# Four staging buffers for the second MoE's weights, and each weight conversion split into two queued steps

## The chip, the cores and the metric

The kernel runs on one core of one Trainium2 chip. The metric is device time in microseconds (us) of one execution, the median of several runs. The engines are named as in the profile: PE is TensorE (matmuls, with PEld for its weight loads), ACT is ScalarE, DVE is VectorE, POOL is GpSimd and SP is SyncE, which here only issues DMAs. Each engine works through its own queue in order; semaphores join the queues.

## What is computed

Three stages in float32: a delta-rule attention, a dense MLP, and a soft mixture of 8 experts in which every token goes through every expert. The change touches the third stage (D = 384, E = 8 experts, F = 1024, N = 3072 tokens).

```
def _moe2_ref(x, w_gate, w1, w2) -> np.ndarray:
    N, D = x.shape
    E = w_gate.shape[1]
    logits = x @ w_gate
    ...
    for e in range(E):
        h = np.maximum(x @ w1[e], 0.0)
        ye = h @ w2[e]
        out += P[:, e:e + 1] * ye
    return out.astype(np.float32)
```

`P` is the gate, normalised over rows and columns eight times (a Sinkhorn iteration).

## The kernel before

**Order of the work.** Attention and the first MLP run interleaved over six time steps of 512 tokens. The second MoE then runs in three passes (`p`) of 1024 tokens (two time steps each), each over 8 experts (`e`), each over 4 groups (`k`) of 256 hidden columns. `groups` lists these 96 triples and `n` numbers them.

**Precision.** Every float32 operand is held as two float16 halves, high and low, and a product is made of three matmuls (high-high, high-low, low-high). A Strassen-like scheme makes each 2x2 block product out of 7 products on sums of blocks; therefore each group's first weights need four sums of blocks beside the six blocks themselves.

**One expert on PE.** `prod` gives each group 11 products of three matmuls of 512 columns (33; 132 for an expert). `second` gives each of 8 token blocks 24 matmuls of 384 columns (192 for an expert). ACT copies out of PSUM (`copied`, L975) and makes high halves of the hidden values (`hi`, L990), DVE adds (`mixed`, L980), makes low halves (`lo`, L994) and accumulates each finished token block into `acc` (`flush`, L1061). For the first expert of a pass `flush` is a plain copy on ACT instead (L1056).

**Preparing weights.** While PE computes the 8 token blocks of one expert, the weights of the next are converted: four tasks `make_w1` and four `make_w2`, in turn, one at each `prep.now()` behind a block's `flush`. A task's raw float32 weights are brought by a DMA from `wc` into a staging tile `stg` (L790 or L807, issued by SP). `make_w1` then has ACT scale them in place (`scaled`, L750), POOL make the four sums (L799, which write into the same tile), ACT write the high half in two pieces (L801) and POOL the low half in two pieces (L802). `make_w2` is a scale, a high half (L813) and a low half (L814). All of ACT's instructions here go through `ordered`, which fixes them in program order; a `stg` tile comes free when POOL's last piece of the task has read it.

**The queue of tasks.** `Stage.fetch` starts loads until two tasks are loaded; `staging` has two buffers. `Stage.step` fetches, converts the oldest loaded task and fetches again. At the last group of an expert (`k == 3`) the tasks of the next expert are added. At the last expert of the first two passes (`edge`) two tasks more are added, which load the next pass's two blocks of `x` (L741, 768 KB each) and split and sum them (`make_xo`: `pair` and the sums in `xsum`, ACT L754, DVE L764 and L755). These instructions of `make_xo` do not go through `ordered`: the scheduler of the framework places them between the others.

**Where PE meets the conversion.** In the next expert's first group, PE makes products in PSUM bank `ph` (`self.x`), ACT copies it (`x1 = copied(self.x, "xc", 1)`), PE goes on with banks `y` and `z`, and then accumulates into `ph` again (`fifth`), for which the copy must have been made. On ACT that copy stands in the queue behind all of the conversions.

Of the kernel before, what the change touches and what calls it, by code (L numbers as in the profile page):

```python
# [8 lines left out]
F32 = mybir.dt.float32  # L9
# [11 lines left out]
NT = S // C  # L21
NP = H // 2
DM = H * D
KD = DM // 128
FF1 = 2048
NF1 = FF1 // 128
E = 8
# [3 lines left out]
TB = B * C  # L31
# [5 lines left out]
W1R, W2R = 6, 8  # L37
# [15 lines left out]
def delta_moe_kernel(ctx: ExitStack, tc: tile.TileContext, k_l, v_l, q_l, beta_l, wa_in, wg, wc, out):  # L53
# [324 lines left out]
    class Background:  # L378
        def __init__(self):
            self.threads = deque()  # L380
            self.active = deque()
            self.credit = 0.0

        def add(self, key, fn, after=()):
            self.threads.append((key, fn, after))
# [34 lines left out]
        def pending(self):  # L420
            return bool(self.active or self.threads)
# [203 lines left out]
    if True:  # L625
# [102 lines left out]
        w1o = [[wr_p.tile([128, 9, 128], F16, name=f"w1{n}{i}") for n in "hl"] for i in range(W1R)]  # L728
        w2o = [[wr_p.tile([128, 2, DM], F16, name=f"w2{n}{i}") for n in "hl"] for i in range(W2R)]
        cst_p = ctx.enter_context(tc.tile_pool(name="cst", bufs=2, side="right", reuse_waits="tile"))  # L730
# [3 lines left out]
        gx = [gx_p.tile([128, KD, TB], F32R, name=n) for n in ("gxh", "gxl")]  # L734

        def staging():
            return cst_p.tile([128, KD * TB], F32, tag="stg", name="stg", bufs=2)

        def load_x(t):
            s = staging().rearrange("p (c n) -> p c n", c=KD)  # L740
            sp.dma_start(out=s, in_=x2_dram[t].rearrange("c p n -> p c n"))  # L741
            return s
# [6 lines left out]
        def scaled(x, col):  # L749
            ordered(act.activation(out=x, in_=x, func=ACTF.Copy, scale=scl[:, col:col + 1]))  # L750

        def pair(hi, lo, src, col):
            sc = scl[:, col:col + 1]
            act.activation(out=hi, in_=src, func=ACTF.Copy, scale=sc)  # L754
            dve.scalar_tensor_tensor(out=lo, in0=src, scalar=sc, in1=hi, op0=ALU.mult, op1=ALU.subtract)  # L755

        def make_xo(s, t):
            i, col, xo = t % 2, 2 * E + t, xos[t // 2 % 2]
            b11, b12 = s[:, 0, 0:256], s[:, 0, 256:512]
            b21, b22 = s[:, 1, 0:256], s[:, 1, 256:512]  # L760
            tt = cst_p.tile([128, 4, 256], F32, tag="xsum", name="xsum", bufs=1)
            for o, x, y in ((tt[:, 0], b12, b11), (tt[:, 1], b22, tt[:, 0]), (tt[:, 2], b22, b12),
                            (tt[:, 3], b21, tt[:, 1])):
                dve.tensor_tensor(out=o, in0=x, in1=y, op=ALU.subtract)  # L764
            for j, src in ((slice(0, 1), s[:, 0:1, 0:256]),
                           (slice(1, 5), s[:, 1:3].rearrange("p c (n k) -> p (c n) k", n=2)), (slice(5, 9), tt)):
                if j.stop - j.start > 1:
                    for n in range(j.start, j.stop):
                        pair(xo[0][:, n, i], xo[1][:, n, i], src[:, n - j.start], col)
                else:  # L770
                    pair(xo[0][:, j.start, i], xo[1][:, j.start, i], src[:, 0], col)
                yield

        groups = [(p, e, k) for p in range(NT // 2) for e in range(E) for k in range(NF2 // 2)]
# [3 lines left out]
        def ordered(ins):  # L778
            e = ins.ins.engine
            if e in last_of:  # L780
                tc.add_manual_dep(ins.ins, last_of[e].ins.name, mybir.DependencyInfo(
                    mybir.DependencyClass.NoSync, mybir.DependencyReason.DATA), reason="as written")
            last_of[e] = ins
# [3 lines left out]
        def load_w1(n):  # L787
            _, e, k = groups[n]
            s = staging()[:, 0:1280].rearrange("p (j f) -> p j f", f=128)
            sp.dma_start(out=s[:, 0:6].rearrange("p (j c) f -> p j (c f)", j=2),  # L790
                         in_=wc[e, 2 * k:2 * k + 2, :, 0:DM].rearrange("j p c -> p j c"))
            return s

        def make_w1(n, s):
            hi, lo = w1o[n % W1R]
            scaled(s[:, 0:6], groups[n][1])
            for o, x, y, op in ((6, 3, 4, ALU.add), (7, 6, 0, ALU.subtract), (8, 0, 3, ALU.subtract),
                                (9, 1, 7, ALU.subtract)):
                pool.tensor_tensor(out=s[:, o], in0=s[:, x], in1=s[:, y], op=op)  # L799
            for j, i in ((slice(0, 3), slice(0, 3)), (slice(3, 9), slice(4, 10))):  # L800
                ordered(act.activation(out=hi[:, j], in_=s[:, i], func=ACTF.Copy))  # L801
                pool.tensor_tensor(out=lo[:, j], in0=s[:, i], in1=hi[:, j], op=ALU.subtract)  # L802
# [6 lines left out]

        def make_w2(n, s):  # L810
            hi, lo = w2o[n % W2R]
            scaled(s, E + groups[n][1])
            ordered(act.activation(out=hi, in_=s, func=ACTF.Copy))  # L813
            pool.tensor_tensor(out=lo, in0=s, in1=hi, op=ALU.subtract)  # L814


        class Stage:
            def __init__(self):
                self.tasks, self.loaded = deque(), deque()

            def add(self, load, make, arg):
                self.tasks.append((load, make, arg))

            def fetch(self):
                while self.tasks and len(self.loaded) < 2:
                    load, make, arg = self.tasks.popleft()
                    self.loaded.append((make, arg, load(arg)))

            def step(self):
                self.fetch()  # L830
                if self.loaded:
                    make, arg, s = self.loaded.popleft()
                    g = make(arg, s)
                    self.fetch()
                    if g:
                        yield from g

            def now(self):
                for _ in self.step():
                    pass  # L840

        prep = Stage()

# [8 lines left out]
        def pre_c():  # L852
            yield from powers(0, NSC, bank)
            for t in (2, 3, 4, 0, 1):
                prep.add(load_x, early_x, t)
                if t > 1:
                    prep.add(load_w1, make_w1, t - 2)
                    prep.add(load_w2, make_w2, t - 2)
            prep.add(load_w1, make_w1, 3)
            prep.add(load_w2, make_w2, 3)  # L860
            prep.fetch()
            yield
            yield
            while prep.loaded:
                yield from prep.step()
                yield
            last_of.clear()
# [86 lines left out]
            for c in range(KD):  # L954
                parts(g5[0][:, c], g5[1][:, c], s[:, c], dve)

        prep.add(load_x, late_x, NT - 1)
        prep.now()
        bgq.add("sink", sinkhorn)

# [23 lines left out]
        class Group:  # L984
# [24 lines left out]
            def second(self):  # L1009
                prod(self.x, self.n, [(7, 7)], False)  # L1010
                mixed(self.x, self.q, out=self.q)
                self.c[1, 0] = mixed(self.w, self.q)
# [54 lines left out]
        for n, (p, e, k) in enumerate(groups):  # L1067
            g = Group(n)
            edge = e == E - 1 and p < NT // 2 - 1
            if k == NF2 // 2 - 1:  # L1070
                for j in range(n + 1, min(n + 5, len(groups))):
                    if edge and j < n + 3:
                        prep.add(load_x, lambda t, s: make_xo(s, t), 2 * p + 1 + j - n)
                    prep.add(load_w1, make_w1, j)
                    prep.add(load_w2, make_w2, j)
                prep.fetch()

            g.first(prev)
            if prev:
                prev.second()  # L1080
            g.third(prev)
            if prev:
                prev.fourth()
            g.fifth(prev)
            prev = g
            if k < NF2 // 2 - 1:
                continue
            prev = None
            ps = [ye_p.tile([128, 512], F32, tag="ye", name="ye") for _ in range(2)]
            g.hi(0, 1)  # L1090
            second(ps[0], n, 0, range(NF2 - 2))
            g.second()
            g.lo(0, 1)
            g.hi(1, 0)
            g.lo(1, 0)
            second(ps[1], n, 1, range(NF2 - 2))
            g.fourth()
            g.hi(1, 1)
            g.lo(1, 1)
            for blk in range(2 * B):  # L1100
                if blk < 2:
                    second(ps[blk], n, blk, range(NF2 - 2, NF2))
                    y = ps[blk]
                else:
                    y = ye_p.tile([128, 512], F32, tag="ye", name="ye")
                    second(y, n, blk, range(NF2))
                flush(y, p, e, blk)
                for _ in range(2 if edge and blk < 2 else 1):
                    prep.now()
# [45 lines left out]
```

## Time and profile before

| what | value |
|---|---|
| median of 3 runs | 2574.31 us (2574.07 to 2576.93) |
| the profiled execution: its own time | 2581.06 us |
| its span (first to last instruction) | 2579.3 us |
| mean granted PE clock in it | 0.938 of full speed |
| PE matmul busy | 2315.1 us (90% of the span) |
| ACT busy | 1395.7 us (54%) |
| DVE busy | 1330.6 us (52%) |
| POOL busy | 849.7 us (33%) |

Durations below come from the profiled execution; its own time is 6.75 us above the median of the runs. A busy share is an average over the whole span: the second MoE begins at about 945 us and takes the rest.

### The profile page before, as it was taken

Reading aid. Unit: us, or ns where it says so; the run is one execution under the profiler, and the core shown is the slowest. Engines: PE = TensorE matmul, PEld = TensorE weight load, DVE = VectorE, ACT = ScalarE, POOL = GpSimd, SP = SyncE. Lnnn points to the kernel's source line nnn. Section 1 sums busy time; section 2 is a strip of 40 time slices with the busy share of each in tenths; the row PEclk is TensorE's granted clock in tenths of the full one; section 3 lists DMA queues with packets and bytes.
Section 4 is the critical chain, followed back from the end, with each engine's and each line's share of the span. In section 5 each row is a group of like instructions: output and inputs, shape, how many; then the busy total and the mean of one; then the engine's idle time right before and its main releaser. Section 6 shows DMA issues by size and latency. Waiting matters only on the chain.

```text
span 2579.3 us, 36179 instructions
## 1 busy us (share of the span) xinstructions
PE 2315.1 (90%) x13842; PEld 1454.1 (56%) x13842; DVE 1330.6 (52%) x2529; ACT 1395.7 (54%) x2445; POOL 849.7 (33%) x966
## 2 busy tenths in 40 slices
PE   6888899899999888898999799999998899999998
PEld 5776778677778654444454344444444444444454
DVE  8667867676642557434444545444434443444444
ACT  6887665656554645445445555454555554454543
POOL 5435211333322313333333233333333333333330
PEclk7678999999899999999999899999999999999999
DMA  3355665555443631111111221111112311111110
GB/s 114 129 167 174 220 211 164 196 175 189 149 137 113 226 106 50 50 50 42 44 50 48 63 61 38 49 50 49 50 50 62 86 50 50 50 49 39 49 50 25
DMA packets 127133, 240.05 MB, mean 93 GB/s; under 512 B 13552, under 2 KB 98160, under 8 KB 126960
## 3 DMA queue, kind: packets, MB, share of 16 engines
q1 hardware_dynamic: 126960, 237.75, 29.6%
q8 instruction: 108, 1.77, 0.3%
q14 instruction: 65, 0.53, 0.1%
HBM read 215.59 MB, written 22.02 MB: 92 GB/s over the span
## 4 chain that ended last, share of the span: by engine, by line
PE 52%; ACT 15%; DMA 11%; POOL 11%; DVE 7%; issue 3%; POOLq 0%; ACTq 0%; SPq 0%; DVEq 0%
PE ye L1048 13%; PE ph L965 12%; DMA stg<-wc 7%; PE w L965 6%; POOL stg L799 5%; POOL w1l L802 5%; PE ph L550 4%; PE y L965 3%; PE z L965 3%; PE po L602 3%; ACT stg L750 3%; DMA wraw<-wc 2%; PE y_ps L355 2%; PE w_ps L346 2%; ACT w1h L801 1%
## 5 line engine op out<-in xcount | busy, mean ns | idle before, releaser
L799 POOL TENSOR_TENSOR stg<-stg 128x128 f32<-128x128 f32 x384 | 171.2, 467 | 1080.1 <-ACT stg L750 1051.3
L965 PEld LDWEIGHTS <-w1h 128*128 128x128 f16 x2112 | 213.1, 101 | 394.9 <-issue 174.2
L1061 DVE SCALAR_TENSOR_TENSOR acc<-ye,pm,acc 128x384 f32<-128x384 f32 x168 | 103.4, 617 | 430.9 <-PE ye L1048 430.9
L965 PE MATMUL ph<-xoh,w1h 128*128 128x512 f16 x480 | 190.5, 397 | 127.6 <-ACT xc L975 122.0
L750 ACT ACTIVATE stg<-stg,scl 128x768 f32<-128x768 f32 x192 | 177.7, 926 | 222.8 <-DMA stg<-wc 222.8
L802 POOL TENSOR_TENSOR w1l<-stg,w1h 128x384 f16<-128x384 f32 x192 | 245.8, 1280 | 7.7
L602 PE MATMUL po<-gh,w 128*128 128x512 f32 (+1 forms) x600 | 218.0, 407 | 4.9 <-ACT gh L590 4.9
L801 ACT ACTIVATE w1h<-stg 128x384 f16<-128x384 f32 x192 | 131.1, 683 | 137.5 <-POOL stg L799 134.5
L550 PE MATMUL ph<-x1h,w 128*128 128x512 f32 (+1 forms) x600 | 186.7, 418 | 7.6 <-DMA w<-wa_scratch 4.8
L965 PE MATMUL ph<-xol,w1h 128*128 128x512 f16 x480 | 190.0, 396 | 0.0
L965 PE MATMUL ph<-xoh,w1l 128*128 128x512 f16 x480 | 189.3, 394 | 0.0
L980 DVE SCALAR_TENSOR_TENSOR q<-ph,q 128x512 f32<-128x512 f32 x192 | 131.4, 685 | 108.2 <-PE ph L965 108.2
L965 PEld LDWEIGHTS <-w1l 128*128 128x128 f16 x1056 | 107.0, 101 | 136.8 <-issue 21.8
L980 DVE SCALAR_TENSOR_TENSOR c<-y,xc 128x512 f32<-128x512 f32 x96 | 66.4, 691 | 192.7 <-ACT xc L975 187.6
L814 POOL TENSOR_TENSOR w2l<-stg,w2h 128x768 f16<-128x768 f32 x96 | 157.6, 1642 | 20.3 <-ACT w2h L813 15.8
L975 ACT ACTIVATE xc<-ph 128x512 f32<-128x512 f32 x96 | 56.8, 592 | 186.6 <-DVE c L980 186.6
L550 PEld LDWEIGHTS ph<-x1h,w 128*128 128x128 f32 x600 | 113.9, 203 | 31.4 <-DVE leak L588 3.8
L602 PEld LDWEIGHTS po<-gh,w 128*128 128x128 f32 x600 | 115.5, 196 | 28.0 <-ACT gh L590 7.9
L602 PE MATMUL po<-gl,w 128*128 128x512 f32 (+1 forms) x300 | 121.5, 405 | 6.5 <-POOL gl L592 5.5
L588 DVE TENSOR_TENSOR leak<-leak,ph 128x512 f32<-128x512 f32 (+1 forms) x100 | 66.1, 661 | 116.5 <-ACT leak L587 115.9
L592 POOL TENSOR_TENSOR gl<-leak,gh 128x512 fp32r<-128x512 f32 x48 | 62.1, 1293 | 184.8 <-ACT gh L590 171.9
L587 ACT ACTIVATE leak<-ph 128x512 f32<-128x512 f32 (+1 forms) x100 | 57.7, 577 | 74.8 <-PE ph L550 72.5
(299 smaller groups left out, 6052.1 us busy)
## 6 DMA issues: line engine op xcount, KB each, us to landing
w<-wa_scratch SPq DMA_DIRECT2D x100, 768.0 KB, 4.6
stg<-wc SPq DMA_DIRECT2D x192, 384.0 KB, 3.4
wraw<-wc SPq DMA_DIRECT2D x128, 192.0 KB, 3.2
raw<-wa SPq DMA_DIRECT2D x48, 256.0 KB, 3.0
wa_scratch<-cvp SPq DMA_DIRECT2D x48, 256.0 KB, 2.5
stg<-x_scratch SPq DMA_DIRECT2D x10, 768.0 KB, 4.5
q<-q_l SPq DMA_DIRECT2D x24, 256.0 KB, 3.3
v<-v_l SPq DMA_DIRECT2D x24, 192.0 KB, 2.4
```

Source lines behind the costliest of these rows:

```text
L550: pe.matmul(out=ps, lhsT=wt[:, c * 128:(c + 1) * 128], rhs=xx[:, c], start=(n == 0), stop=(n == 3 * KD - 1))
L588: dve.tensor_tensor(out=g, in0=g, in1=ps, op=ALU.max)
L602: pe.matmul(out=po[c][:, cols], lhsT=wt[:, DM + c * 128:DM + (c + 1) * 128], rhs=xx, start=(i == 1 and m == 0), stop=(i == n and m == 2), ...
L750: ordered(act.activation(out=x, in_=x, func=ACTF.Copy, scale=scl[:, col:col + 1]))
L799: pool.tensor_tensor(out=s[:, o], in0=s[:, x], in1=s[:, y], op=op)
L801: ordered(act.activation(out=hi[:, j], in_=s[:, i], func=ACTF.Copy))
L802: pool.tensor_tensor(out=lo[:, j], in0=s[:, i], in1=hi[:, j], op=ALU.subtract)
L814: pool.tensor_tensor(out=lo, in0=s, in1=hi, op=ALU.subtract)
L965: ordered(pe.matmul(out=ps, lhsT=w[:, a], rhs=x[:, b].rearrange("p s k -> p (s k)"), start=first, stop=i == 2 and (a, b) == terms[-1], ski ...
L980: ordered(dve.scalar_tensor_tensor(out=c, in0=bank, scalar=sign * HS, in1=y, op0=ALU.mult, op1=ALU.add))
L1048: ordered(pe.matmul(out=ps[:, 0:DM], lhsT=xx[:, o:o + 128], rhs=wt, start=(f == 0 and i == 0), stop=(f == NF2 - 1 and i == 2), skip_group_ ...
L1061: dve.scalar_tensor_tensor(out=a, in0=y, scalar=pm[:, t * B + b, e:e + 1], in1=a, op0=ALU.mult, op1=ALU.add)
```

## The change

Two things are changed. `staging` gets four buffers, and `fetch` loads until four tasks are loaded or begun. And each task is cut in two: `begin` issues the scale and, for first weights, the four sums; `make` issues the high and low halves. `step` issues `make` of the task that has been begun, then `begin` of the next one, and fetches behind that.

```
@@ -734,7 +734,7 @@
         gx = [gx_p.tile([128, KD, TB], F32R, name=n) for n in ("gxh", "gxl")]
 
         def staging():
-            return cst_p.tile([128, KD * TB], F32, tag="stg", name="stg", bufs=2)
+            return cst_p.tile([128, KD * TB], F32, tag="stg", name="stg", bufs=4)
 
         def load_x(t):
             s = staging().rearrange("p (c n) -> p c n", c=KD)
@@ -791,12 +791,14 @@
                          in_=wc[e, 2 * k:2 * k + 2, :, 0:DM].rearrange("j p c -> p j c"))
             return s
 
-        def make_w1(n, s):
-            hi, lo = w1o[n % W1R]
+        def sums_w1(n, s):
             scaled(s[:, 0:6], groups[n][1])
             for o, x, y, op in ((6, 3, 4, ALU.add), (7, 6, 0, ALU.subtract), (8, 0, 3, ALU.subtract),
                                 (9, 1, 7, ALU.subtract)):
                 pool.tensor_tensor(out=s[:, o], in0=s[:, x], in1=s[:, y], op=op)
+
+        def make_w1(n, s):
+            hi, lo = w1o[n % W1R]
             for j, i in ((slice(0, 3), slice(0, 3)), (slice(3, 9), slice(4, 10))):
                 ordered(act.activation(out=hi[:, j], in_=s[:, i], func=ACTF.Copy))
                 pool.tensor_tensor(out=lo[:, j], in0=s[:, i], in1=hi[:, j], op=ALU.subtract)
@@ -809,35 +811,55 @@
 
         def make_w2(n, s):
             hi, lo = w2o[n % W2R]
-            scaled(s, E + groups[n][1])
             ordered(act.activation(out=hi, in_=s, func=ACTF.Copy))
             pool.tensor_tensor(out=lo, in0=s, in1=hi, op=ALU.subtract)
 
 
+        def scale_w2(n, s):
+            scaled(s, E + groups[n][1])
+
+        def none(arg, s):
+            pass
+
+        W1, W2 = (load_w1, sums_w1, make_w1), (load_w2, scale_w2, make_w2)
+
+
         class Stage:
             def __init__(self):
-                self.tasks, self.loaded = deque(), deque()
-
-            def add(self, load, make, arg):
-                self.tasks.append((load, make, arg))
+                self.tasks, self.loaded, self.ready = deque(), deque(), deque()
+
+            def add(self, how, arg):
+                self.tasks.append((how, arg))
 
             def fetch(self):
-                while self.tasks and len(self.loaded) < 2:
-                    load, make, arg = self.tasks.popleft()
-                    self.loaded.append((make, arg, load(arg)))
+                while self.tasks and len(self.loaded) + len(self.ready) < 4:
+                    (load, begin, make), arg = self.tasks.popleft()
+                    self.loaded.append((begin, make, arg, load(arg)))
+
+            def begin(self):
+                if self.loaded:
+                    begin, make, arg, s = self.loaded.popleft()
+                    begin(arg, s)
+                    self.ready.append((make, arg, s))
 
             def step(self):
                 self.fetch()
-                if self.loaded:
-                    make, arg, s = self.loaded.popleft()
+                if not self.ready:
+                    self.begin()
+                if self.ready:
+                    make, arg, s = self.ready.popleft()
                     g = make(arg, s)
-                    self.fetch()
+                    self.begin()
                     if g:
                         yield from g
+                    self.fetch()
 
             def now(self):
                 for _ in self.step():
                     pass
+
+            def pending(self):
+                return bool(self.tasks or self.loaded or self.ready)
 
         prep = Stage()
 
```

The tasks of the early part (`pre_c`), the late `x` task and those at the end of an expert are handed over in the new form; tasks that load `x` have an empty `begin`:

```
@@ -852,16 +874,16 @@
         def pre_c():
             yield from powers(0, NSC, bank)
             for t in (2, 3, 4, 0, 1):
-                prep.add(load_x, early_x, t)
+                prep.add((load_x, none, early_x), t)
                 if t > 1:
-                    prep.add(load_w1, make_w1, t - 2)
-                    prep.add(load_w2, make_w2, t - 2)
-            prep.add(load_w1, make_w1, 3)
-            prep.add(load_w2, make_w2, 3)
+                    prep.add(W1, t - 2)
+                    prep.add(W2, t - 2)
+            prep.add(W1, 3)
+            prep.add(W2, 3)
             prep.fetch()
             yield
             yield
-            while prep.loaded:
+            while prep.pending():
                 yield from prep.step()
                 yield
             last_of.clear()
```

**What moves on the engines.** In an expert that is neither the first nor the last of a pass, ACT and POOL carry out the same instructions in the same order as before (scale, high, high, scale, high and so on; sums, low, low, low and so on), and SP issues the same loads in the same order; only the waits differ. Three places do move.

The first is ACT in the first expert of the second pass, from the last hidden value `h71h` on (`acc<-ye` is the copy of a token block, `stg<-stg,scl` a scale, `w1h` and `w2h` high halves). Before:

```order
L990 ACTIVATE h71h<-cx 128x512
L1056 ACTIVATE acc<-ye 128x384
L750 ACTIVATE stg<-stg,scl 128x768
L801 ACTIVATE w1h_9554<-stg 128x384
L801 ACTIVATE w1h_9554<-stg 128x768
L1056 ACTIVATE acc<-ye 128x384
L750 ACTIVATE stg<-stg,scl 128x768
L813 ACTIVATE w2h_9574<-stg 128x768
```

And of the change:

```order
L1012 ACTIVATE h71h<-cx 128x512
L1078 ACTIVATE acc<-ye 128x384
L750 ACTIVATE stg<-stg,scl 128x768
L803 ACTIVATE w1h_9554<-stg 128x384
L803 ACTIVATE w1h_9554<-stg 128x768
L750 ACTIVATE stg<-stg,scl 128x768
L1078 ACTIVATE acc<-ye 128x384
L814 ACTIVATE w2h_9574<-stg 128x768
```

Each scale has moved from behind the next block's copy to ahead of it.

The second is ACT at the end of the conversions ahead of the last expert of the first pass (`xoh` is made by `make_xo`, nine pieces for each of the two blocks of `x`; `xc<-ph` is the copy that PE needs). Before:

```order
L750 ACTIVATE stg<-stg,scl 128x768
L813 ACTIVATE w2h_9580<-stg 128x768
L754 ACTIVATE xoh_9548<-stg,scl 128x256 x3
L975 ACTIVATE xc<-ph 128x512
L754 ACTIVATE xoh_9548<-stg,scl 128x256 x2
L754 ACTIVATE xoh_9548<-xsum,scl 128x256 x3
```

And of the change:

```order
L750 ACTIVATE stg<-stg,scl 128x768
L814 ACTIVATE w2h_9580<-stg 128x768
L754 ACTIVATE xoh_9548<-stg,scl 128x256 x5
L754 ACTIVATE xoh_9548<-xsum,scl 128x256 x4
L754 ACTIVATE xoh_9548<-stg,scl 128x256 x5
L754 ACTIVATE xoh_9548<-xsum,scl 128x256 x4
L997 ACTIVATE xc<-ph 128x512
```

Before, the second block's nine pieces stood among the last expert's own conversions, one expert later; now all eighteen stand ahead of the copy.

The third is DVE at the same place (`acc<-ye` accumulates a token block, `xsum` and `xol` belong to `make_xo`, `c<-y,xc` is the first sum of the next expert). Before:

```order
L1061 SCALAR_TENSOR_TENSOR acc<-ye,pm,acc 128x384 x6
L764 TENSOR_TENSOR xsum<-stg 128x256 x2
L1061 SCALAR_TENSOR_TENSOR acc<-ye,pm,acc 128x384
L764 TENSOR_TENSOR xsum<-stg,xsum 128x256
L755 SCALAR_TENSOR_TENSOR xol_9549<-stg,scl,xoh_9548 128x256
L764 TENSOR_TENSOR xsum<-stg,xsum 128x256
L755 SCALAR_TENSOR_TENSOR xol_9549<-stg,scl,xoh_9548 128x256
L980 SCALAR_TENSOR_TENSOR c<-y,xc 128x512
```

And of the change:

```order
L1083 SCALAR_TENSOR_TENSOR acc<-ye,pm,acc 128x384 x4
L764 TENSOR_TENSOR xsum<-stg 128x256 x2
L764 TENSOR_TENSOR xsum<-stg,xsum 128x256 x2
L755 SCALAR_TENSOR_TENSOR xol_9549<-stg,scl,xoh_9548 128x256 x3
L1083 SCALAR_TENSOR_TENSOR acc<-ye,pm,acc 128x384
L755 SCALAR_TENSOR_TENSOR xol_9549<-stg,scl,xoh_9548 128x256 x2
L755 SCALAR_TENSOR_TENSOR xol_9549<-xsum,scl,xoh_9548 128x256 x4
L764 TENSOR_TENSOR xsum<-stg 128x256 x2
L764 TENSOR_TENSOR xsum<-stg,xsum 128x256
L1083 SCALAR_TENSOR_TENSOR acc<-ye,pm,acc 128x384
L764 TENSOR_TENSOR xsum<-stg,xsum 128x256
L755 SCALAR_TENSOR_TENSOR xol_9549<-stg,scl,xoh_9548 128x256 x5
```

Three accumulations that stood ahead of all or most of `make_xo` now stand inside it.

## Rows read from the trace of the kernel before

**Rows 1.** The page: the chain that ended last, shares of the span by engine.

```profile
PE 52%; ACT 15%; DMA 11%; POOL 11%; DVE 7%; issue 3%; POOLq 0%; ACTq 0%; SPq 0%; DVEq 0%
```

**Rows 2.** Waits of PE from 1050 us on: total us, times, longest.

```profile
PE ph L965 <- ACT xc L975: 122.0, 22, 11.2
PE ye L1048 <- ACT acc L1056: 3.3, 4, 0.9
```

**Rows 3.** ACT in one expert's conversions: start, us, instruction, idle before it.

```profile
1189.07 0.92 ACT L750 ACTIVATE stg<-stg,scl 128x768 f32<-128x768 f32 x1
...
1191.92 0.84 ACT L801 ACTIVATE w1h<-stg 128x768 f16<-128x768 f32 x1 [1.37 <-POOL stg L799]
1192.67 0.92 ACT L750 ACTIVATE stg<-stg,scl 128x768 f32<-128x768 f32 x1
1193.62 0.84 ACT L813 ACTIVATE w2h<-stg 128x768 f16<-128x768 f32 x1
1197.82 0.94 ACT L750 ACTIVATE stg<-stg,scl 128x768 f32<-128x768 f32 x1 [3.35 <-DMA stg<-wc]
...
1222.59 0.58 ACT L975 ACTIVATE xc<-ph 128x512 f32<-128x512 f32 x1
```

**Rows 4.** POOL in the same conversions.

```profile
1198.83 1.82 POOL L799 TENSOR_TENSOR stg<-stg 128x128 f32<-128x128 f32 x4 [2.65 <-ACT stg L750]
1200.60 2.64 POOL L802 TENSOR_TENSOR w1l<-stg,w1h 128x384 f16<-128x384 f32 x2
1203.30 1.64 POOL L814 TENSOR_TENSOR w2l<-stg,w2h 128x768 f16<-128x768 f32 x1
```

**Rows 5.** The DMA view from 1100 us on: all loads, from issue to landing.

```profile
DMA to landing us min/median/max: 3.0/3.4/5.1
```

**Rows 6.** The chain around the wait and after it: start, us, work.

```profile
1187.87 13.66 PE ye L1048 x84
...
1227.22 1.30 PE ph L965 x6
...
1248.58 0.65 PE ph L965 x3
```

**Rows 7.** Windows: length, busy PE, PEld, DVE, ACT, POOL, PEclk, DMA share, GB/s.

```profile
1216.10:1223.20 7.10, 0.36 (x2) 0.08 (x1) 0.00 (x1) 4.46 (x6) 4.68 (x7) 0.79 0.27 85
1223.20:1227.20 4.00, 3.98 (x10) 1.46 (x10) 1.38 (x2) 1.60 (x3) 1.20 (x1) 0.51 0.68 187
1227.20:1249.20 22.00, 22.00 (x104) 9.98 (x102) 16.89 (x27) 13.05 (x24) 0.00 (x0) 1.00 0.01 3
```

**Rows 8.** The chain: the first `w` product of three experts.

```profile
1291.44 2.56 PE w L965 x6
...
1572.24 2.56 PE w L965 x6
1906.09 2.56 PE w L965 x6
```

**Rows 9.** `make_xo`'s pieces on ACT in the timeline: three, and nine later.

```profile
1428.09 1.30 ACT L754 ACTIVATE xoh<-stg,scl 128x256 f16<-128x256 f32 x3 [4.53 <-DMA stg<-x_scratch]
...
1474.93 2.10 ACT L754 ACTIVATE xoh<-stg,scl 128x256 f16<-128x256 f32 x5 [4.51 <-DMA stg<-x_scratch]
1476.94 1.69 ACT L754 ACTIVATE xoh<-xsum,scl 128x256 f16<-128x256 f32 x4
```

**Rows 10.** The timeline: POOL's sums and DVE early on; DVE in the conversions.

```profile
905.17 4.82 POOL L799 TENSOR_TENSOR stg<-stg 128x128 f32<-128x128 f32 x4 [14.47 <-ACT stg L750]
904.99 1.66 DVE L755 SCALAR_TENSOR_TENSOR xol<-xsum,scl,xoh 128x256 f16<-128x256 f32 x4
1201.56 0.62 DVE L1061 SCALAR_TENSOR_TENSOR acc<-ye,pm,acc 128x384 f32<-128x384 f32 x1 [3.28 <-PE ye L1048]
```

**Rows 11.** Two stretches ahead of the steady part, columns as in the windows above.

```profile
840.00:944.00 104.00, 92.39 (x382) 68.43 (x382) 54.49 (x101) 54.43 (x95) 28.11 (x29) 0.92 0.55 186
944.00:1050.00 106.00, 93.85 (x489) 47.22 (x488) 78.45 (x169) 56.78 (x95) 24.19 (x28) 1.00 0.18 50
```

More of the change, by code (lines that the diff above doesn't have):

```diff
@@ L955, in late_x @@
                 parts(g5[0][:, c], g5[1][:, c], s[:, c], dve)
-        prep.add(load_x, late_x, NT - 1)
+        prep.add((load_x, none, late_x), NT - 1)
         prep.now()
@@ L1072, in delta_moe_kernel @@
                     if edge and j < n + 3:
-                        prep.add(load_x, lambda t, s: make_xo(s, t), 2 * p + 1 + j - n)
-                    prep.add(load_w1, make_w1, j)
-                    prep.add(load_w2, make_w2, j)
+                        prep.add((load_x, none, lambda t, s: make_xo(s, t)), 2 * p + 1 + j - n)
+                    prep.add(W1, j)
+                    prep.add(W2, j)
                 prep.fetch()
```

## The prediction

> **What bounds the kernel now.** I began with the chain that ended last. PE holds only 52% of it; ACT, DMA and POOL hold 37% between them [rows 1], although PE is busy for 90% of the span. So PE is the bound for most of the time and hands over to the others in places. The list of PE's waits says which places: in the second MoE, PE waits 22 times, 122.0 us in all, for the copy `xc` that ACT makes of PSUM bank `ph` [rows 2]. There are 24 experts and so 23 passages from one to the next; the wait is there once per passage, with one exception (the first, where the Sinkhorn iteration holds PE up).
>
> The timeline of ACT across one passage tells why. Let zero be 1189.07, the start of the first scale. A pair of tasks (first weights, second weights) takes 8.75 us, from the scale at 1189.07 to the one at 1197.82, and 3.35 us of that is ACT waiting for a load; `xc` starts at 1222.59, which is 33.5 after zero [rows 3]. PE's own way to the point where it needs the copy is shorter. From 1187.87 it makes 156 matmuls of the token blocks at 13.66/84 = 0.1626 us each, 25.37 us [rows 6], and then 15 matmuls for banks `ph`, `y` and `z`. Their price comes from the stretch that runs without a gap, from 1227.22 to the end of the piece at 1248.58, 1249.23: 19 pieces with 102 matmuls in 22.01 us, 0.2158 each [rows 6]. So PE is ready at 1187.87 + 25.37 + 3.24 = 1216.48, which is 27.4 after zero, and the window shows it nearly idle from 1216.10 to 1223.20 (0.36 us busy) [rows 7]. The wait costs twice: in the 4.00 us after it the granted clock is 0.51, the level of 1.2 GHz, and in the next 22.00 us it is 1.00, 2.4 GHz [rows 7]. Half of those 4 us is lost as well.
>
> An expert's work is 132 x 0.2158 + 192 x 0.1626 = 28.49 + 31.22 = **59.71 us**. From the `w` product at 1572.24 to that at 1906.09 lie five experts, 66.77 us each [rows 8]. So **7.06 us per ordinary passage** is wait and half clock.
>
> **The load goes out earlier.** With two buffers the load of the next first weights can only go out when POOL has read the last of the current ones; then come the landing, the scale, the sums and POOL again, one behind the other. With four, the loads of two pairs are in flight before the first block is done, and the third pair's first load goes out when POOL has finished the first pair's first weights: 0.95 + 1.82 + 2.64 = 5.4 after zero [rows 3, 4]. It lands at 8.8 with the median of 3.4 us and at 10.5 with the maximum of 5.1 [rows 5]. What needs it is the third pair's scale, which comes at 11.4 (below). So none of ACT's waits for `wc` should stay, with 0.9 to 2.6 us to spare.
>
> **What then sets the pace.** POOL's own work in a pair is 1.82 + 2.64 + 1.64 = 6.10 us [rows 4]. The way through both engines is as long: sums done, second high piece (0.75 to the next start), scale (0.95), high half (0.84) [rows 3], then POOL's low half 1.64 and the next sums 1.82, 6.00, and a few hundredths at each hand-off. I take 6.15 for a pair; 6.10 is the lower bound, and today's 8.75 the upper one. ACT is done with the first pair at 1193.62 + 0.75 - 1189.07 = 5.3, and with the fourth at 5.3 + 3 x 6.15 = **23.75** instead of 33.5. The `ph` product is done on PE at 27.4 - 12 x 0.2158 = 24.8, so ACT is free first, and PE can have its copy at 25.4, two microseconds before it wants it. Counted on the conversions, the spare time is 27.4 - 0.6 - 23.75 = 3.0 us: the pair could take 7.15 before PE waited. The ordinary passages lose their whole 7.06. I count 16: the 22 of [rows 2] less three at each of the two changes of pass.
>
> **The split into two steps.** In ordinary experts it moves nothing on ACT, POOL or SP (the order is the same), so I give it nothing there. In the first expert of a pass each scale comes ahead of the next block's copy. Four waits of PE for such a copy, 3.3 us in all [rows 2], are the upper bound of a gain; the lower bound is that ACT's copies come late by one scale, 0.95 us, which conversions that run ahead of PE's 3.90 us per block can bear. They are inside the next sum.
>
> **The changes of pass.** From 1291.44 to 1572.24 are four experts, 280.80 us [rows 8]; one is ordinary, which leaves 214.03 for three whose work is 179.13, a loss of 34.9 (the third of these ends with the first expert of the new pass). What stays of it: all eighteen pieces of `make_xo` now stand on ACT ahead of the copy `xc`. The second block's load takes the buffer of the last second weights, which POOL has read at 25.5; ACT's wait of 4.53 us behind such a load [rows 9] puts its landing at 30.1; nine pieces take 2.10 + 1.69 = 3.8 [rows 9], and the copy 0.6. That is 34.5 against 27.4, a wait of 7.1, and I add 2 for the half clock behind it as in [rows 7]. DVE makes its part of `make_xo` while POOL still works on the last pair. Early in the trace the same kinds of instructions met, and POOL's four sums took 4.82 us beside DVE's `xol`, against 1.82 [rows 4, 10]; the lower bound here is nothing, the upper one 3 us for each of POOL's last two jobs, and I take 2. So 11 stays (7 to 17), and each change of pass gains 34.9 - 11 = 23.9.
>
> This is where a rule of the Trainium skill bears on the change. Its page "SBUF — State Buffer", section "SBUF: two separate sides", says that a DVE instruction with two SBUF inputs and a GpSimd instruction that reads SBUF exclude each other for the whole instruction. The stretched sums agree with it. [...]
>
> **Early parts.** From 840 to 944 us the same tasks run beside the last step of the first MLP, and from 944 to 1050 the first expert and the Sinkhorn iteration: PE is idle for 11.6 and 12.2 us [rows 11]. Loads land earlier there too, but the order of many instructions changes, and no row says which way. The gain is bounded by about 12 (half of the idle time), the loss by as much; I take nothing.
>
> **Sum.** 16 x 7.06 = 113.0, and 2 x 23.9 = 47.8: 160.8 us. The profiled execution would go from 2581.06 to 2420; its span lies 1.8 under that time. It stands 6.75 above the median of the runs, so I take the difference from the median: 2574.3 - 160.8 = **2413 us**.
>
> **Rivals.**
> *A shorter wait stays at each passage.* The pair takes more than 7.15 us, since scale, sums and halves depend on each other across two engines with no room. At 7.45, half way to today's pace, ACT is free at 27.65 and the copy done at 28.25; PE waits 0.85, with up to 2 more for the clock. 16 x 0.85 to 2.85 is 14 to 46 us, which gives 2427 to 2459, say 2443. Against it: each duration in the sum is measured beside the same neighbours.
> *DVE holds POOL up in every passage.* Six accumulations of 0.62 us fall into the conversions. If POOL stood still for each, 3.7 us would be added, 0.7 more than there is to spare: 16 x 0.7 = 11, so 2424. Against it: one of them runs at 1201.56 beside POOL's low pieces, which take 2.64 as they do elsewhere [rows 4, 10]. (The Trainium skill's same page, section "Who interferes with whom", exempts a DVE instruction with at most one SBUF input; the accumulation reads one from PSUM.)
> *The change does not do what it says.* The loads still go out late, because SP, one queue for all of them, sits behind another wait. Then all stays as it is, 2574. Against it: in these passages SP has only loads, in the order in which buffers come free.
> *Slower.* In the early part the stage loads share SP's queue with the loads of the first MLP's weights. If a stage load waited there for a buffer long enough to starve PE in the stretch from 840 to 944, that time would be added. It decides from 161 us on, more than the stretch is long; at 170 the time would be 2583. I see nothing for it.
>
> **Chances.** The forecast 0.77, the shorter wait 0.13, POOL held up 0.05, no effect 0.03, slower 0.02. The range takes 12 us off for the early parts and 8 for the changes of pass, to 2393, and on the other side 12 for each of these and a small remaining wait, to 2440; that leaves out the upper half of the shorter wait, and the last two cases. Within 0.2% (5 us, about what a measurement of this kernel can tell from no change) falls only the case without effect. Faster 0.95, same 0.03, slower 0.02.
>
> **What would show it.** In the changed kernel's list of PE's waits, that for `xc` should be down from 22 to the two at the changes of pass, of about 7 us each. ACT should have no wait for `stg<-wc` in the passages; its wait for POOL's sums stays. `xc` should start about 24.8 after the first scale, `w` products should lie 59.7 to 60 apart, and the granted clock should stay at 1.00 across ordinary passages. I am wrong if PE still waits there: then a pair takes over 7.15 us, and ACT's idle time in front of the scale or of the second high piece says whether a load or POOL is late.

## The result, and the profile after

The changed kernel takes 2416.61 us (median of 4 runs, 2412.23 to 2423.62) against 2575.62 us (4 runs) for the kernel before beside it: a ratio of 0.938, with a 95% interval of 0.9349 to 0.9412. Forecast were 2413 us and a range of 2393 to 2440.

The waits of PE from 1045 us on, where the second expert's token blocks begin (total us, times, longest), to be read against [rows 2]:

```profile
PE ye L1070 <- DVE acc L1083: 16.0, 2, 8.0
PE ye L1070 <- ACT acc L1078: 1.3, 2, 0.7
```

The wait for `xc` is gone from all 22 passages, the two at the changes of pass included. What is left is another wait, twice 8.0 us, for DVE's accumulation.

The page: the granted PE clock in 40 slices; the chain, against [rows 1]; and ACT's scale, with the idle time ahead of it behind the second bar, which was 222.8 us in the page of before:

```profile
PEclk7679899999999999999999999999999999999999
...
PE 71%; ACT 10%; DVE 8%; DMA 4%; POOL 3%; issue 3%; SPq 0%; POOLq 0%; ACTq 0%; DVEq 0%
...
L750 ACT ACTIVATE stg<-stg,scl 128x768 f32<-128x768 f32 x192 | 176.7, 920 | 0.7 <-DMA stg<-wc 0.7
```

The chain is PE's for 71%, not 52%, and ACT's scale waits for the loads of `wc` for 0.7 us in all. The first `w` product of an expert, in the chain of the changed kernel (as [rows 8]; between them lie one expert, two, one, one and one):

```profile
1146.06 1.29 PE w L987 x6
...
1205.75 1.29 PE w L987 x6
...
1325.13 1.29 PE w L987 x6
...
1395.64 1.29 PE w L987 x6
...
1455.33 1.29 PE w L987 x6
...
1515.85 1.29 PE w L987 x6
```

Ordinary experts lie 59.69 us apart (1205.75 - 1146.06), the change of pass costs 70.51, and the first expert of the new pass 60.52. The whole difference of the two profiled executions, 2579.3 - 2421.9 = 157.4 us of span, splits at a point that both traces have, the first `ph` product among the second expert's token blocks (1050.0 before, 1052.8 after): from there to PE's last matmul (2575.6 and 2418.2) the changed kernel is 160.2 faster, and it is 2.8 slower ahead of that.

One ordinary passage, which in the kernel before took the times of [rows 3, 4]: first ACT, then POOL.

```profile
1356.79 0.92 ACT L750 ACTIVATE stg<-stg,scl 128x768 f32<-128x768 f32 x1
...
1359.64 0.84 ACT L803 ACTIVATE w1h<-stg 128x768 f16<-128x768 f32 x1 [1.37 <-POOL stg L798]
1360.39 0.92 ACT L750 ACTIVATE stg<-stg,scl 128x768 f32<-128x768 f32 x1
...
1362.09 0.92 ACT L750 ACTIVATE stg<-stg,scl 128x768 f32<-128x768 f32 x1
...
1365.71 0.84 ACT L803 ACTIVATE w1h<-stg 128x768 f16<-128x768 f32 x1 [2.15 <-POOL stg L798]
```

```profile
1363.86 1.82 POOL L798 TENSOR_TENSOR stg<-stg 128x128 f32<-128x128 f32 x4
1365.64 2.64 POOL L804 TENSOR_TENSOR w1l<-stg,w1h 128x384 f16<-128x384 f32 x2
1368.33 1.65 POOL L815 TENSOR_TENSOR w2l<-stg,w2h 128x768 f16<-128x768 f32 x1
1369.94 1.82 POOL L798 TENSOR_TENSOR stg<-stg 128x128 f32<-128x128 f32 x4
```

The scale at 1362.09 has no bracket behind it: where [rows 3] shows 3.35 us of waiting for a load, there is none. POOL now runs without a break, and a pair takes 1369.94 - 1363.86 = 6.08 us. What ACT waits for is POOL's sums (159.7 us, 84 times, from 1090 us on), and PE's list shows no wait that comes of it. `xc` starts 24.83 us after the first scale in the ordinary passages; about 24.8 was forecast.

These are the conversions ahead of the last expert of the first pass, and the two blocks of `x` for the next pass are split at their end. That is what is called a change of pass here. Its chain, and the timelines of DVE and POOL at the same place:

```profile
1374.38 4.54 DMA stg<-x_scratch
...
1378.95 3.87 DVE xsum L764 x3
...
...
1384.46 0.54 DVE acc L1083
...
1385.04 6.72 PE ye L1070 x24
```

```profile
1378.95 3.52 DVE L764 TENSOR_TENSOR xsum<-stg 128x256 f32<-128x256 f32 x2 [9.05 <-DMA stg<-x_scratch]
...
1384.38 0.61 DVE L1083 SCALAR_TENSOR_TENSOR acc<-ye,pm,acc 128x384 f32<-128x384 f32 x1
...
1387.39 0.76 DVE L764 TENSOR_TENSOR xsum<-stg 128x256 f32<-128x256 f32 x2
```

```profile
1377.78 2.63 POOL L804 TENSOR_TENSOR w1l<-stg,w1h 128x384 f16<-128x384 f32 x2
1380.48 1.72 POOL L815 TENSOR_TENSOR w2l<-stg,w2h 128x768 f16<-128x768 f32 x1
```

DVE stands at the head of its queue with a sum of the `x` block whose load goes out at 1374.38, when POOL has read the third pair's first weights; behind that sum stands the accumulation that frees a PSUM bank for the next token block, and PE waits for it, from 1377.0 to 1385.0. Of these 8.0 us, 2.8 are the two sums that take 3.52 us beside POOL and 0.76 without it. Then the clock: windows of the changed kernel (us, busy time of each engine, granted clock, DMA share, GB/s).

```profile
1362.00:1376.00 14.00, 14.00 (x88) 8.44 (x87) 1.33 (x3) 9.26 (x13) 13.52 (x16) 1.00 0.44 120
1376.00:1385.00 9.00, 1.04 (x7) 0.49 (x5) 6.01 (x9) 6.21 (x12) 5.97 (x8) 0.73 0.61 193
1385.00:1390.00 5.00, 4.96 (x16) 2.31 (x16) 4.97 (x13) 2.84 (x8) 0.00 (x0) 0.50 0.57 186
```

The 24 matmuls behind the wait take 6.72 us, 2.8 more than 24 at 0.1625; with the wait of 8.0 that is 10.8, the whole 70.51 - 59.69.

### The profile page after: what moved, and what is told of

It reads as the page before. It is cut to its first block, busy times and chain, and to the rows that moved or that the text cites. A ratio compares the mean times of both kernels' runs of the same rounds, so it can differ in the third digit from the quotient of the medians.

```text
span 2421.9 us, 36086 instructions
## 1 busy us (share of the span) xinstructions
PE 2264.9 (94%) x13842; PEld 1440.1 (59%) x13842; DVE 1332.6 (55%) x2529; ACT 1392.4 (57%) x2445; POOL 853.0 (35%) x966
## 4 chain that ended last, share of the span: by engine, by line
PE 71%; ACT 10%; DVE 8%; DMA 4%; POOL 3%; issue 3%; SPq 0%; POOLq 0%; ACTq 0%; DVEq 0%
PE ye L1070 28%; PE ph L987 12%; PE w L987 5%; PE y L987 5%; PE z L987 5%; PE ph L550 4%; PE po L602 4%; DMA wraw<-wc 2%; PE y_ps L355 2%; PE w_ps L346 2%; ACT a_d L214 2%; ACT x L280 1%; POOL stg L798 1%; DMA x_scratch<-x2o 1%; ACT p L296 1%
## 5 line engine op out<-in xcount | busy, mean ns | idle before, releaser
L987 PEld LDWEIGHTS <-w1h 128*128 128x128 f16 x2112 | 206.5, 98 | 250.2 <-issue 11.0
L987 PE MATMUL ph<-xoh,w1h 128*128 128x512 f16 x480 | 181.9, 379 | 8.1 <-DVE q L1002 2.6
L987 PE MATMUL ph<-xol,w1h 128*128 128x512 f16 x480 | 181.9, 379 | 0.0
L987 PE MATMUL ph<-xoh,w1l 128*128 128x512 f16 x480 | 181.9, 379 | 0.0
L592 POOL TENSOR_TENSOR gl<-leak,gh 128x512 fp32r<-128x512 f32 x48 | 62.2, 1296 | 183.5 <-ACT gh L590 160.2
```

The lines of the kernel that those rows point to most:

```text
L987: ordered(pe.matmul(out=ps, lhsT=w[:, a], rhs=x[:, b].rearrange("p s k -> p (s k)"), start=first, stop=i == 2 and (a, b) == terms[-1], ski ...
```

## Experiments

Two explanations were to be told apart first. **A**: only the earlier loads, that is the buffers, give the gain. **B**: the split into two steps gives part of it. Then A's own numbers were tried, and what is left at the changes of pass.

**The changed kernel again** (e_again; with the last group e_again2).

> The changed kernel itself, unchanged, as a yardstick on the same chip as the next three. Every theory: 2416 us, within 5.

Measured: 2417.98 us, ratio 0.9382 (0.9356 to 0.9409).

> The changed kernel once more, beside the other two on one chip: 2417 us (2408 to 2424), experts 59.69 us apart, 10.8 us more at each change of pass.

Measured: 2424.28 us, ratio 0.9402 (0.938 to 0.9424). That is just past the range. From the point of the second expert named above to PE's last matmul it is 1365.4, 1365.5 and 1365.4 us in the three profiled executions; the second MoE's first product starts at 936.3, 925.6 and 937.6. So the scatter between executions lies ahead of the second MoE, and the distances between experts tell small effects better than the medians do.

**Buffers alone** (e_buffers): the kernel before, with its one-step tasks.

```
-  return cst_p.tile([128, KD * TB], F32, tag="stg", name="stg", bufs=2)
+  return cst_p.tile([128, KD * TB], F32, tag="stg", name="stg", bufs=4)
-  while self.tasks and len(self.loaded) < 2:
+  while self.tasks and len(self.loaded) < 4:
```

> Four staging buffers and four loads ahead, each conversion in one step as before. Theory A (only the earlier loads count, since ACT, POOL and SP keep their order in ordinary experts): PE's waits for xc are gone, experts 59.7 us apart, 2416 us, at most 4 more for the copies in the first expert of a pass. Theory B (the scale and sums queued ahead bring the gain): the passages keep most of their 7 us, 2560 to 2575.

Measured: 2418.74 us, ratio 0.9382 (0.9353 to 0.9411): the changed kernel's time. Experts lie 59.69 us apart; the first experts of the second and third pass take 59.70 and 59.69, where the changed kernel takes 60.52, and the experts behind them 59.86, where it takes 59.69. PE's waits:

```profile
PE ye L1048 <- DVE acc L1061: 15.9, 2, 8.0
PE ph L965 <- DVE c L980: 1.1, 1, 1.1
```

**The split alone** (e_split): the changed kernel with `bufs=2` and the limit `< 2`.

> Each conversion in two steps, but two staging buffers and two loads ahead as before. Theory A: nothing is gained, a pair of tasks takes 8.75 us on ACT, 22 waits of PE for xc stay, 2574 us within 10. Theory B: most of the gain is there, 2416 to 2440.

Measured: 2577.02 us, ratio 1.0003 (0.9991 to 1.0015). The wait of [rows 2] is back, and so is the idle time ahead of the scale on the page:

```profile
PE ph L987 <- ACT xc L997: 124.7, 22, 11.7
```

```profile
L750 ACT ACTIVATE stg<-stg,scl 128x768 f32<-128x768 f32 x192 | 177.8, 926 | 232.0 <-DMA stg<-wc 231.4
```

A holds and B falls. The split gives nothing in the ordinary passages. Set beside e_buffers, the changed kernel loses 0.8 us in each of the two first experts of a pass, whose token blocks are copied by ACT behind a scale, and has 0.17 of it back in the expert behind.

**Three buffers** (e_three): the changed kernel with `bufs=3` and the limit `< 3`.

> The changed kernel with three staging buffers and three loads ahead. Theory A, from the landing times: the second pair's second weights are loaded into the first buffer from 5.4 us after the first scale on, land at 8.8 (10.5 at most), and are wanted at 9.75, so ordinary passages run without a wait, as with four: 2416 us within 10. Rival (the fourth buffer is needed): a pair takes over 7.15 us, PE waits at every passage, 2430 or more.

Measured: 2410.13 us, ratio 0.9364 (0.933 to 0.9397); experts 59.69 us apart. From the same point to the end it takes 1364.7 us, the changed kernel's 1365.4 within a microsecond. The interval of its ratio overlaps the changed kernel's; its profiled execution, the fastest of its runs (2399.92), starts the second MoE early (first product at 915.0), and no run shows why. ACT's scale waits for a load for 3.5 us in all of the span. In the stretch that the change was made for, three buffers do what four do.

**A longer pair** (e_pool1, e_pool3): one or three more sums on POOL in each first-weights task, to see how long a pair may take (`range(3)` in e_pool3). The repeated sum writes the value that is there already.

```
                 pool.tensor_tensor(out=s[:, o], in0=s[:, x], in1=s[:, y], op=op)
+            for _ in range(1):
+                pool.tensor_tensor(out=s[:, 9], in0=s[:, 1], in1=s[:, 7], op=ALU.subtract)
```

> The changed kernel with one of POOL's sums of each first-weights task done a second time (0.455 us more for a pair). If a passage has 3 us to spare, as worked out, ACT is free at 23.5 + 4 x 0.455 = 25.3 after the first scale and the copy is done before PE wants it: no wait, 2417 us within 5. If there is no room, four times 0.455 us stand at each of 22 passages: 2457.

Measured: 2469.54 us, ratio 0.9589 (0.9547 to 0.9631), a clear miss. Experts lie 62.13 us apart, and PE waits for `xc` again:

```profile
PE ph L989 <- ACT xc L999: 35.8, 20, 1.9
```

POOL's timeline shows that the edit did more than was meant:

```profile
1107.42 1.81 POOL L798 TENSOR_TENSOR stg<-stg 128x128 f32<-128x128 f32 x4 [32.70 <-ACT stg L750]
1109.19 0.92 POOL L806 TENSOR_TENSOR w1l<-stg,w1h 128x384 f16<-128x384 f32 x1
1110.06 0.45 POOL L800 TENSOR_TENSOR stg<-stg 128x128 f32<-128x128 f32 x1
1111.47 1.65 POOL L806 TENSOR_TENSOR w1l<-stg,w1h 128x768 f16<-128x768 f32 x1 [0.95 <-ACT w1h L805]
...
1114.77 1.81 POOL L798 TENSOR_TENSOR stg<-stg 128x128 f32<-128x128 f32 x4
```

The scheduler put the extra sum (L800) behind the first low piece. ACT's second high piece needs that sum, and POOL's second low piece needs the high piece, so POOL stands idle for 0.95 us in each pair. The pair takes 1114.77 - 1107.42 = 7.35 us, not 6.5.

> The same with three such sums more (1.365 us more for a pair). With 3 us to spare, ACT is free at 29.0, the copy done at 29.6, and PE waits 2.2 us at 22 passages, with up to 2 us more each for the clock: 2465 to 2510. With no room, 22 x 5.5: 2538. With much more room than 3 us: 2417.

Measured: 2606.96 us, ratio 1.0109 (1.0072 to 1.0145). The sums of the pairs start at 1142.47, 1150.89, 1159.33 and 1167.76: 8.43 us for a pair. Ordinary experts lie 67.5 to 68.5 apart. The time is above every case forecast, since the pair was to take 7.45 us.

By the prediction's account four pairs may take 3.0 us more before PE waits. At 7.35 us they take 4 x 1.27 = 5.1 more, which leaves a wait of 2.1; PE waits 35.8/20 = 1.8. At 8.43 it is 4 x 2.35 - 3.0 = 6.4; in that passage PE stands still for 6.2. So the account is not refuted by the miss, but its free part had not been tried. That is the next run.

**The extra sum in its place** (e_sum): GpSimd's instructions kept in written order.

```
+                for _ in range(2 if o == 9 else 1):
+                    ordered(pool.tensor_tensor(out=s[:, o], in0=s[:, x], in1=s[:, y], op=op))
```

The low pieces of both kinds of task go through `ordered` as well.

> The changed kernel with the last of GpSimd's four sums of a W1 conversion made twice, and GpSimd's sums and low pieces kept in written order, so that the fifth sum stands with the others and not behind the first low piece as in e_pool1. Theory A (a pair of conversions may take 1.07 us longer, 7.15 us for 6.08, before the copy that TensorE waits for is late): the pair takes 6.08 + 0.46 = 6.54 us, four of them 1.8 us more than now, under the 3.0 us to spare; TensorE waits for no copy, the experts are 59.7 us apart and the time is that of the changed kernel, 2417 us (2408 to 2424). Theory B (there is nothing to spare; e_pool1 cost what it did for the sum itself): 1.8 us at each of 20 passages, 2453 us.

Measured: 2418.51 us, ratio 0.939 (0.9362 to 0.9417). POOL's rows, with five sums:

```profile
1300.61 2.35 POOL L799 TENSOR_TENSOR stg<-stg 128x128 f32<-128x128 f32 x5 [33.24 <-ACT stg L750]
1302.91 2.65 POOL L805 TENSOR_TENSOR w1l<-stg,w1h 128x384 f16<-128x384 f32 x2
1305.61 1.64 POOL L816 TENSOR_TENSOR w2l<-stg,w2h 128x768 f16<-128x768 f32 x1
1307.21 2.34 POOL L799 TENSOR_TENSOR stg<-stg 128x128 f32<-128x128 f32 x5
```

A pair takes 6.60 us, four of them 2.1 more than in the changed kernel, and the experts still lie 59.69 apart, with no wait for `xc`. The changes of pass (71.2 and 71.8) and the first experts of a pass (61.1) are longer than in the changed kernel, by 3.6 us in all. So a pair may take 6.60 us without a wait and 7.35 us not; the prediction's limit of 7.15 lies between the two.

**The changes of pass** (e_ordered, e_parts, e_best). If the rest there is DVE's accumulation behind sums that wait for `x`, it goes when the `x` blocks come earlier or DVE's order is fixed. In e_ordered the blocks stay where they are, and `make_xo` and the accumulations go through `ordered`:

```
-            dve.scalar_tensor_tensor(out=a, in0=y, scalar=pm[:, t * B + b, e:e + 1], in1=a, op0=ALU.mult, op1=ALU.add)
+            ordered(dve.scalar_tensor_tensor(out=a, in0=y, scalar=pm[:, t * B + b, e:e + 1], in1=a, op0=ALU.mult, op1=ALU.add))
```

> The changed kernel with only the order of the split of x fixed: its pieces and the accumulations stay in program order, so both blocks are split in the last expert of a pass, from loads that landed long before. No 8 us wait for an accumulation; but nine pieces twice hold ACT up (about 28.7 after the first scale instead of 23.5 and a wait of 1 to 2 us there) and an accumulation twice by 1 to 3 us: 5 us of the 11.7 stay, 2404.

Measured: 2442.2 us, ratio 0.9476 (0.9446 to 0.9506): missed, it is slower than the changed kernel. The changes of pass take 75.21 and 74.09 us, and most other experts 60.50. DVE and POOL at the first change:

```profile
1424.12 4.42 DVE L755 SCALAR_TENSOR_TENSOR xol<-xsum,scl,xoh 128x256 f16<-128x256 f32 x4
1428.47 0.60 DVE L1083 SCALAR_TENSOR_TENSOR acc<-ye,pm,acc 128x384 f32<-128x384 f32 x1
```

```profile
1423.01 2.69 POOL L804 TENSOR_TENSOR w1l<-stg,w1h 128x384 f16<-128x384 f32 x2 [1.76 <-ACT w1h L803]
1425.66 1.81 POOL L815 TENSOR_TENSOR w2l<-stg,w2h 128x768 f16<-128x768 f32 x1
```

In written order a whole `x` block stands ahead of the second accumulation, and it runs beside POOL: four `xol` pieces take 4.42 us. In the changed kernel the same four take 1.67 at 1385.69, where POOL has nothing to do. PE stands still for 5.7 and 3.2 us behind the two blocks.

In e_parts each of the experts 5 and 6 gets one block, in three parts between the token blocks 0, 1 and 2, with the same `ordered`:

```
-            edge = e == E - 1 and p < NT // 2 - 1
+            edge = e in (E - 3, E - 2) and p < NT // 2 - 1
...
+                if edge and blk < 3:
+                    if blk == 0:
+                        xg = prep.step()
+                    next(xg, None)
```

> The changed kernel, with the next pass's blocks of x split one each in the experts two and three before the pass ends instead of both in the last, in program order on ACT and DVE, their pieces in three parts between the token blocks. If the 11.7 us that stay at each change of pass come from DVE's accumulation standing behind pieces that wait for a load of x, they go: experts 60 to 62 us apart everywhere, 2417 - 2 x 10 = 2397. If the load of x or POOL's work beside it costs the time wherever it stands, 2417.

Measured: 2408.16 us, ratio 0.935 (0.9318 to 0.9382). The changes of pass cost no more than other experts, but nearly every expert now takes 60.50, 0.81 more, so that the time lies between the two that were expected. Waits of PE, and the chain at one such place:

```profile
PE ye L1070 <- DVE acc L1083: 15.3, 21, 1.2
```

```profile
1357.31 0.69 DVE h71l L1016
1358.00 0.54 DVE acc L1083
```

In written order `h71l` stands ahead of the first accumulation; the changed kernel's scheduler had put it behind (the accumulation at 1356.60, `h71l` at 1357.14). The token blocks 0 to 3 don't read it. So e_best is e_parts with that line moved:

```
             g.hi(1, 1)
-            g.lo(1, 1)
             for blk in range(2 * B):
...
                 flush(y, p, e, blk)
+                if blk == 0:
+                    g.lo(1, 1)
```

> The changed kernel, with three more edits: one x block in each of the experts 5 and 6 of a pass in place of both in the expert 7, in three parts between its token blocks; the copies of these blocks, the sums ahead of them and the accumulations kept in written order; and h71l written behind the first accumulation, where the changed kernel's order has it too. Theory A (what is left at a change of pass is DVE's accumulation behind the sums that wait for the x load; the 0.81 us at every expert of e_parts was the first accumulation behind h71l): every expert 59.7 us apart, the changes of pass too (60.0 at most), so 10.5 us less at each of the two than in the changed kernel, and 21 times 0.81 less than in e_parts: 2396 us, 2388 to 2402. Theory B (the 0.81 us came from keeping DVE's accumulations in a row at all, wherever h71l stands): experts 60.5 apart and 2408 as e_parts. Theory C (at a change of pass something else comes to light, the copy xc or the first pair): 5 us or more stay at each, 2405 or more.

Measured: 2395.18 us, ratio 0.929 (0.9265 to 0.9314), the fastest kernel of the study; e_again2, beside it, took 2424.28. PE's waits from 1045 us on, and a window that holds the split of both `x` blocks for the second pass (DVE's pieces of it start at 1290.0 and 1350.3):

```profile
PE ye L1070 <- ACT acc L1078: 1.3, 2, 0.7
PE ph L987 <- ACT q L997: 1.0, 4, 0.3
```

```profile
1284.00:1375.00 91.00, 90.74 (x511) 49.80 (x509) 53.90 (x83) 56.01 (x92) 47.79 (x55) 1.00 0.26 75
```

Experts lie 59.69 us apart, over the changes of pass too, except 60.26 behind the experts 5 and 6, a little more than the 60.0 of theory A, and 60.52 in the first experts of a pass. From the same point to the end it takes 1346.6 us, 18.8 less than the changed kernel: 10.8 + 10.3 from the changes of pass, less four times 0.57. The other 10 us of the medians' difference lie ahead of that and are not explained: it came to that point at 1044.7 and e_again2 at 1053.8, while the changed kernel itself has been there at 1042.5. So the distances between experts bear theory A out, and that the median hit 2396 is in part luck.

## Why the prediction was right, step by step

**Ordinary passages: mechanism and size as forecast.** 7.06 us per passage were to go, and an expert to take 59.71; it takes 59.69. ACT's waits for loads fell from 222.8 to 0.7 us, the pair takes 6.08 us for 6.15, and the runs with longer pairs put the wait where the 3.0 us of spare time are used up. e_buffers and e_split show that the buffers alone do this.

**Changes of pass: the amount right, the place wrong.** 11 us were to stay at each, and 10.8 and 10.3 did. But the step "That is 34.5 against 27.4, a wait of 7.1" failed: there is no wait for `xc` there at all. PE stops about 20 us after the first scale, among the token blocks. Its half on ACT held: the last piece of `make_xo` ends at 1390.9, 34.1 after the first scale, so that a copy could be done at 34.7. What failed is PE's 27.4: held up by the 8.0 us and by the half clock behind them, PE had its `ph` product done only at 35.6. So the late copy is there, hidden behind the earlier wait. By these numbers it would come out if DVE's wait alone were taken away; no run tried that. I had followed `make_xo` on ACT and not on DVE's queue, where a sum that waits for the `x` load holds up the accumulation. The trace before had a sign of it: its list of waits has `ye` waiting for DVE's `acc` for 6.1 us in two places, a line that I passed over:

```profile
PE ye L1048 <- DVE acc L1061: 6.1, 2, 3.1
```

That the sum came out is luck: a wait of 8.0 at another place for 7.1, a half clock of 2.8 for 2, and no time of POOL's on top where I had 2.

**POOL hindered by DVE: the other way round.** The two sums that took 0.76 us at 1387.39 took 3.52 at 1378.95, while POOL's low pieces beside them took 2.63 and 1.72, hardly more than the 2.65 and 1.64 that they take alone. Here DVE stood still. The Trainium skill's page "SBUF — State Buffer", section "SBUF: two separate sides", says that of two such instructions the one that starts first goes through and the other is blocked until it ends. The trace agrees: POOL's low pieces began at 1377.78 and DVE's sum at 1378.95, whereas in [rows 10] DVE's pieces began at 904.99 and POOL's sums, which were stretched, at 905.17. I had charged POOL with 2 us; the runs show nothing there and 2.8 us on DVE, inside the wait of 8.0.

**The split: a small loss, not nothing.** The lower bound that I gave named what happens: the copies come late by a scale. But the cover that I named for it (3.90 us per block) does not hide all of it. Beside e_buffers it costs 0.83 us in each of the two first experts, and the wait for ACT's `acc` in the changed kernel's list, 0.7 us in each, is most of it; e_buffers has no such wait.

**Early parts: no effect is shown.** The changed kernel's profiled execution was 2.8 us later there, well inside the 12 either way and less than what executions of one kernel differ by. (The stretch to 1050 holds more than the first expert: PE begins the second expert's products at 1016.3 before and at 1019.4 after.)

**The rivals.** The shorter wait did not stay; its condition, a pair over 7.15 us, came about in e_pool1 and e_pool3, and then the wait came. The accumulations do not hold POOL up in ordinary passages (6.08 us is its own work). The loads did go out early, and PE's idle time early on hardly changed: 10.9 and 13.7 us in the two stretches of [rows 11], for 11.6 and 12.2.

What stays open is what moves the start of the second MoE between executions, by 12 us in the changed kernel alone (925.6 to 937.6).

## What to carry to other kernels

When an engine waits for a copy, look at what else stands in the queue of the engine that makes it: here a load's latency, paid several times in a row on ACT, cost PE its time, and buffers alone took it away. When a wait is removed, ask in every in-order queue what stands behind the next late load; a scheduler may place an instruction that waits ahead of one that another engine needs, and then writing the order by hand helps only if every line stands where it should. An experiment that adds an instruction has to be read in the order that the engines ran it, or it tests something else.

## What the runs showed of the hardware

In the changed kernel's clock records PE is granted full speed (2.4 GHz) from 998 us until its first long wait, in which it stood still from 1377.0 to 1385.0; at each of the two changes of pass about 10 us are at 0.50 (1.2 GHz), and nothing else up to PE's last matmul. Beside POOL, one of DVE's sums takes 1.86 us where the median is 0.42, as the view of the tile `xsum` has it (count, least, median and longest in ns):

```profile
L764 DVE TENSOR_TENSOR xsum<-stg x12: 389/422/1855, 889.2 to 1877.3; 128x256 f32<-128x256 f32 x12
```
